# Attention and two feed-forward layers on one core: weight conversions moved between steps, key slots laid out anew

## The chip, the cores and the metric

The kernel runs on one core of a Trainium2 chip. The metric is the device time of one execution in microseconds (us). Before the change the median of three runs is 629.02 us (628.22 to 630.41).

## What is computed

Attention with a window and sinks, then two feed-forward layers, each over the 1536 tokens that the one before gives (2 batches of 768):

```python
scores = scale * np.matmul(q, k.transpose(0, 1, 3, 2))
keep = (pos[None, :] < n_sink) | ((rel >= 0) & (rel < window))
scores = np.where(keep, scores, -1e9); a = softmax(scores)
x = np.matmul(a, v)                       # 8 heads of 64, written as [1536, 512]
x = softplus(x @ w_in) @ w_out            # 512 -> 2048 -> 512
y = ((h := x @ w2_in) * np.clip(h + 3, 0, 6) / 6) @ w2_out
```

With the inputs, n_sink is 4 and window is 128. The weights arrive as 64-bit floats.

## The kernel before

**Attention.** The tokens are cut into 12 groups g of 128 (i = g % 6 within a batch), and the 8 heads into two quads. Step n of the loop at L603 handles group n // 2, quad n % 2, for n from 0 to 23; steps 24 to 26 finish what is in flight. Work is a pipeline: step n issues the scores of n on TensorE (PE), the transposes of the probabilities of n-1, on odd steps the transposes of a finished group's output (`turn_x`), and the products with the values of n-2 (`apply`). VectorE (DVE) adds the mask and takes the minimum (`exps`, L500), ScalarE (ACT) exponentiates, and DVE and ACT copy transposed probabilities out of PSUM (`copies`). A group's output is divided by its sums (`normalise`, DVE, L557), turned (PE) and stored as a high part (ACT, L568) and a low part (DVE, L572), since the feed-forward products take each factor as a sum of two parts.

**Keys.** `keys` holds for each block i one slot of 144 columns: 64 keys, 16 columns for the sinks, 64 keys. A query row needs the last 64 keys of the block before, its own block and the sinks, and for half of the rows the first 64 keys of the block before. `spread_sinks` (GpSimd, POOL) copies the sinks to all slots once per batch. Blocks with i == 0 need no block before; their scores are taken in halves of 64 keys (L480).

**Weights.** A "half" (`Weights.half`, L87) converts one 512 KB piece of a weight matrix from 64-bit to two 32-bit parts: three DVE instructions (L97, L100, L103), one on ACT (L107), one on POOL (L108). `fetch` keeps up to four pieces loading ahead. `HALVES` says behind which steps a half is put: steps 3, 5 to 23, eleven in all. The names are w_c_io, c the column block of 128, io 0 for w_in and 1 for w_out.

**Feed-forward.** Steps 24 to 26 already hold the first-layer products of column blocks c = 0, 1 and 2 for tokens 0 to 511 (`products`, 12 matmuls of 512 columns each). `activate` (softplus, L155) runs over ACT, POOL and DVE; its DVE instruction L175 sets the PSUM buffer of the product free, of which there are three. `stage_b` (L188) multiplies with w_out, again 12 matmuls. From `ffn.run` on, `filler` puts the rest of the halves behind the activations of c = 4 to 14.

**What sets the order.** The whole part up to `ffn.run(0, FIXED)` stands under `in_order`: each engine executes its instructions in the order in which the program writes them. So a DVE instruction that waits holds all DVE work behind it. Loads go out on SyncE's queue (SP) in program order, each one waiting until the load eight places ahead has landed.

Of the kernel before, what the change touches and what calls it, by code (L numbers as in the profile page):

```python
# [8 lines left out]
F32 = mybir.dt.float32  # L9
# [5 lines left out]
ALU = mybir.AluOpType  # L15
# [3 lines left out]
P = 128  # L19
NEG = 1.0e9  # L20
MAXSINK = 16
HQ = P // 2
SLOTW = P + MAXSINK
YW = HQ + MAXSINK
PW = P + YW
TB = 2
HALVES = (3, 5, 7, 9, 11, 13, 15, 17, 19, 21, 23)
WARM = 22
FIXED = 4

# [338 lines left out]
def banded_attention(ctx, tc, qT_d, kT_d, v, ident, NSv, Wv, xT, psa, isq, w, ffn, flags):  # L369


    nc = tc.nc
    B, H, D, S = qT_d.shape
# [3 lines left out]
    NQ = 2 * NG  # L377
# [10 lines left out]
    def fetch(g):  # L388
        b, i = divmod(g, NB)
        s = st.setdefault(g, {})  # L390
        s["q"] = thr.tile([P, NP, P], F32, tag="q", name=f"q_{g}")
        for ps in (slice(0, NP),) if g else (slice(0, NP // 2), slice(NP // 2, NP)):
            for t, src, eng in ((0, qT_d, nc.sync), (1, kT_d, nc.sync if g else nc.scalar)):
                src = src[b].rearrange("(p t) d s -> (t d) p s", t=2)[:, ps, i * P : (i + 1) * P]
                if t == 0:
                    eng.dma_start(s["q"][:, ps], src)
                else:
                    for r in range(2):
                        c0 = r * (HQ + MAXSINK)
                        eng.dma_start(keys[:, ps, i, c0 : c0 + HQ], src[:, :, r * HQ : (r + 1) * HQ])  # L400

    def fetch_v(g):
        b, i = divmod(g, NB)
        s = st.setdefault(g, {})
        s["vx"] = thr.tile([P, H, D], F32, tag="vx", name=f"vx_{g}")
        lo = i * P - (HQ if i else 0)
        nc.sync.dma_start(s["vx"], v[b, lo : lo + P])
        if i:
            s["vy"] = thr.tile([YW, 2, H, D], F32, tag="vy", name=f"vy_{g}")
            lo = (i - 1) * P  # L410
            nc.sync.dma_start(s["vy"][0:HQ, 0], v[b, lo : lo + HQ])
            nc.sync.dma_start(s["vy"][HQ:YW, 0], v[b, 0:MAXSINK])
            lo = i * P + HQ
            nc.sync.dma_start(s["vy"][0:MAXSINK, 1], v[b, 0:MAXSINK])
            nc.sync.dma_start(s["vy"][MAXSINK:YW, 1], v[b, lo : lo + HQ])

    def spread_sinks():

        nc.gpsimd.tensor_copy(
            keys[:, :, :, HQ : HQ + MAXSINK],  # L420
            keys[:, :, 0:1, 0:MAXSINK].to_broadcast([P, NP, NB, MAXSINK]),
        )

# [12 lines left out]
    def masks(i):  # L436

        if i == 0:
            nc.vector.tensor_scalar(out=mt[:, 0:P], in0=rmc, scalar1=0.0, scalar2=hid, op0=ALU.is_lt, op1=ALU.mult)
            nc.vector.tensor_scalar(out=m_zero, in0=rmc, scalar1=Wv, scalar2=hid, op0=ALU.is_ge, op1=ALU.mult)  # L440
            nc.vector.tensor_tensor(out=m_zero, in0=m_zero, in1=mt[:, 0:P], op=ALU.min)
            nc.vector.tensor_scalar(out=mS, in0=col, scalar1=NSv, scalar2=None, op0=ALU.is_ge)
            nc.vector.tensor_tensor(out=m_zero, in0=m_zero, in1=mS, op=ALU.mult)
        elif i == 1:
            nc.vector.tensor_scalar(out=mt, in0=rel, scalar1=0.0, scalar2=hid, op0=ALU.is_lt, op1=ALU.mult)
            nc.vector.tensor_scalar(out=m_gen, in0=rel, scalar1=Wv, scalar2=hid, op0=ALU.is_ge, op1=ALU.mult)
            nc.vector.tensor_tensor(out=m_gen, in0=m_gen, in1=mt, op=ALU.min)
            for r, c0 in ((r0, P + HQ), (r1, P)):
                nc.vector.tensor_scalar(
                    out=m_gen[r, c0 : c0 + MAXSINK], in0=mS[r, 0:MAXSINK], scalar1=hid, scalar2=None, op0=ALU.mult  # L450
                )
            nc.vector.tensor_copy(m_one, m_gen)
            nc.vector.tensor_tensor(
                out=m_one[r0, P : P + HQ], in0=m_gen[r0, P : P + HQ], in1=mS[r0, 0:HQ], op=ALU.mult
            )
            nc.vector.memset(m_one[r0, P + HQ : PW], hid)

    def scores(n):
        g, quad = divmod(n, 2)
        i = g % NB  # L460
        s = st[g]
        if quad == 0:
            s["sum"] = two.tile([P, H], F32, tag="sum", name=f"sum_{g}")
            s["mx"] = two.tile([P, H], F32, tag="mx", name=f"mx_{g}")
        s["P", quad] = two.tile([P, 4, PW], F32, tag="P", name=f"P_{n}")
        s["s", quad] = [psa.tile([P, 2, 256], F32, tag="s", name=f"s_{n}_{t}") for t in range(2)]
        for pp in range(2):
            p = quad * 2 + pp
            if i == 0:
                parts = [None]  # L470
            else:
# [104 lines left out]
    def keep_busy(n):  # L576
# [17 lines left out]
    nc.vector.tensor_scalar(out=rel[:, 0:P], in0=rmc, scalar1=float(HQ), scalar2=None, op0=ALU.add)
    nc.vector.tensor_scalar(
        out=rel[r0, P : P + HQ], in0=rmc[r0, 0:HQ], scalar1=float(P), scalar2=None, op0=ALU.add
    )
    nc.vector.memset(rel[r0, P + HQ : PW], 0.0)
    nc.vector.memset(rel[r1, P : P + MAXSINK], 0.0)
    nc.vector.tensor_scalar(  # L600
        out=rel[r1, P + MAXSINK : PW], in0=rmc[r1, 0:HQ], scalar1=float(-HQ), scalar2=None, op0=ALU.add
    )
    for n in range(NQ + 3):  # L603
        g, quad = divmod(n, 2)
        new, old, older = n < NQ, 0 <= n - 1 < NQ, 0 <= n - 2 < NQ
        late = n >= NQ
        ready = n // 2 - 2 if n % 2 == 0 and n >= 4 else None
        turned = (n - 5) // 2 if n % 2 and n >= 5 else None
        if new:
            scores(n)  # L610
        else:
            ffn.products("w1", 0, n - NQ)
        if n == 0:
            keep_busy(6)
        if old:
            transposes(n - 1)
        if turned is not None:
            turn_x(turned)
        if older:
            apply(n - 2)  # L620
        if late and ready is not None:
            normalise(ready)
        if new:
            for hh in range(4):
                exps(n, hh)
        if old:
            copies(n - 1, nc.vector)
            copies(n - 1, nc.scalar)
        if ready is not None and not late:
            normalise(ready)  # L630
        if turned is not None:
            store_hi(turned)
        if ready is not None and ready >= 1:
            store_lo(ready - 1)
        if n % 2 == 0 and n >= 2 and n // 2 - 1 < NG:
            inverse(n // 2 - 1)
        if quad == 1 and new:
            if g % NB == 0:
# [133 lines left out]
```

## Time and profile before

| | |
|---|---|
| median of 3 runs | 629.02 us |
| the profiled execution | 628.13 us, span 626.3 us |
| PE matmul busy | 611.6 us, 98% of the span, 3804 instructions |
| DVE / ACT / POOL busy | 322.6 / 329.1 / 206.2 us |
| mean granted TensorE clock | 0.992 |
| L145 and L202, the feed-forward products | 1152 matmuls each, 283.7 and 281.9 us |
| DMA | 50.16 MB; 46603 packets, 15249 of them under 512 B |

Busy is the time an engine spends in instructions, as a sum. The span is the profiled execution from its first to its last instruction, and the time has about 1.8 us around it. PE is almost always busy, so time can be won only where PE waits, where its clock is lower, or where it does work that can be left out.

### The profile page before, as it was taken

What the parts mean: (1) busy time and instruction counts of PE and PEld (TensorE: products, weight loads), DVE (VectorE), ACT (ScalarE), POOL (GpSimd) and SP (SyncE); (2) the same over time, 40 slices, a digit from 0 to 9 for tenths busy, and PEclk for the clock granted to TensorE, in tenths of its full rate; (3) what the DMA queues carried; (4) which work ended last, traced back from release to release, by engine and by line L of the source; (5) the groups of instructions that cost most, each with busy time, mean ns of one, the idle gap of its engine ahead of it and who ended that gap; (6) DMA issues with size and microseconds to landing.
All of it is one profiled execution on the core that took longest, in us unless ns stands there. A gap on an engine that the chain in (4) does not pass through costs nothing.

```text
span 626.3 us, 10133 instructions
## 1 busy us (share of the span) xinstructions
PE 611.6 (98%) x3804; PEld 503.3 (80%) x3804; DVE 322.6 (51%) x693; ACT 329.1 (53%) x715; POOL 206.2 (33%) x170
## 2 busy tenths in 40 slices
PE   9799999899999999999999999999999999999996
PEld 5688887688888888888888888888888888888884
DVE  5699976998424222256999984222322222322221
ACT  4698986787668566566878743222222222322221
POOL 1111215898644444446899941000000000000000
PEclk9899999899999999999999999999999999999998
DMA  7999979100000000025665520000100000100001
GB/s 191 277 282 248 261 250 324 69 1 1 1 1 1 0 1 0 2 75 176 213 197 181 168 67 2 1 1 1 67 1 1 1 0 1 67 1 1 1 1 72
DMA packets 46603, 50.16 MB, mean 80 GB/s; under 512 B 15249, under 2 KB 37777, under 8 KB 46545
## 3 DMA queue, kind: packets, MB, share of 16 engines
q1 hardware_dynamic: 45312, 49.16, 25.5%
q8 instruction: 32, 0.52, 0.3%
q10 hardware_dynamic: 1232, 0.26, 0.2%
q14 instruction: 27, 0.21, 0.1%
HBM read 46.27 MB, written 3.15 MB: 79 GB/s over the span
## 4 chain that ended last, share of the span: by engine, by line
PE 87%; DMA 4%; ACT 3%; DVE 2%; SPq 2%; issue 1%; ACTq 0%; DVEq 0%
PE h_w L145 41%; PE y_w L202 40%; PE pt L518 2%; PE o L542 2%; ACT P L504 2%; DMA raw_w<-in_moe_w_out_dram 1%; DMA vx<-in_v_dram 1%; PE s L487 1%; DMA q<-in_q_dram 1%; DMA raw_w<-in_moe_w_in_dram 1%; DVE xs L500 1%; PE xtr L565 1%; DMA vy<-in_v_dram 0%; ACT w_w L107 0%; PE s L480 0%
## 5 line engine op out<-in xcount | busy, mean ns | idle before, releaser
L145 PE MATMUL h_w<-xT,w_w 128*128 128x512 f32 x1152 | 283.7, 391 | 2.8 <-DVE e_w L175 2.8
L145 PEld LDWEIGHTS h_w<-xT,w_w 128*128 128x128 f32 x1152 | 216.9, 189 | 49.2 <-DVE e_w L175 3.9
L202 PE MATMUL y_w<-g_w,w_w 128*128 128x512 f32 x576 | 143.0, 389 | 0.0
L202 PE MATMUL y_w<-w_w,g_w 128*128 128x512 f32 x576 | 138.9, 389 | 0.0
L202 PEld LDWEIGHTS y_w<-w_w,g_w 128*128 128x128 f32 x576 | 107.9, 188 | 23.2 <-ACT g_w L182 0.4
L202 PEld LDWEIGHTS y_w<-g_w,w_w 128*128 128x128 f32 x576 | 108.0, 188 | 22.8 <-DVE xT L572 0.5
L108 POOL TENSOR_TENSOR w_w<-t_w,w_w 128x512 fp32r<-128x512 f32 x64 | 82.8, 1296 | 88.1 <-ACT w_w L107 82.9
L181 DVE SCALAR_TENSOR_TENSOR h_w<-e_w,h_w 128x512 f32<-128x512 f32 x48 | 33.4, 695 | 89.0 <-ACT e_w L179 89.0
L179 ACT ACTIVATE e_w<-h_w 128x512 f32<-128x512 f32 x48 | 28.7, 599 | 96.0 <-PE h_w L145 94.6
L182 ACT ACTIVATE g_w<-h_w 128x512 fp32r<-128x512 f32 x48 | 28.7, 598 | 91.2 <-PE y_w L202 91.0
L183 DVE SCALAR_TENSOR_TENSOR g_w<-h_w,g_w 128x512 fp32r<-128x512 f32 x48 | 33.2, 691 | 83.7 <-ACT g_w L182 83.7
L171 POOL TENSOR_TENSOR u_w<-u_w,e_w 128x512 f32<-128x512 f32 x48 | 62.1, 1293 | 43.1 <-ACT u_w L170 41.0
L177 POOL TENSOR_TENSOR g_w<-e_w,g_w 128x512 fp32r<-128x512 f32 x48 | 62.1, 1295 | 38.8 <-ACT g_w L176 38.1
L174 DVE SCALAR_TENSOR_TENSOR h_w<-h_w,r_w 128x512 f32<-128x512 f32 x48 | 33.4, 696 | 55.9 <-ACT r_w L172 55.7
L504 ACT ACTIVATE P<-xs,mx 128x208 f32<-128x208 f32 (+1 forms) x96 | 42.6, 447 | 12.5 <-DVE mx L500 12.3
L175 DVE TENSOR_TENSOR e_w<-h_w,u_w 128x512 f32<-128x512 f32 x48 | 33.0, 687 | 31.1 <-POOL u_w L171 30.9
L167 ACT ACTIVATE e_w<-h_w 128x512 f32<-128x512 f32 x48 | 28.4, 592 | 37.1 <-PE h_w L145 31.8
L107 ACT ACTIVATE w_w<-t_w 128x512 fp32r<-128x512 f32 x64 | 39.9, 623 | 13.9 <-DVE t_w L103 13.7
L176 ACT ACTIVATE g_w<-e_w 128x512 fp32r<-128x512 f32 x48 | 30.0, 624 | 26.6 <-DVE e_w L175 16.7
L97 DVE TENSOR_SCALAR m_w<-raw_w 128x512 int32<-128x512 int32 x53 | 36.7, 692 | 8.0 <-DMA raw_w<-in_moe_w_in_dram 3.8
L103 DVE SCALAR_TENSOR_TENSOR t_w<-raw_w,m_w 128x512 int32<-128x512 int32 x53 | 36.2, 683 | 2.9
L100 DVE SCALAR_TENSOR_TENSOR m_w<-raw_w,m_w 128x512 int32<-128x512 int32 x53 | 36.6, 691 | 1.0
(74 smaller groups left out, 452.0 us busy)
## 6 DMA issues: line engine op xcount, KB each, us to landing
raw_w<-in_moe_w_in_dram SPq DMA_DIRECT2D x32, 512.0 KB, 4.4
raw_w<-in_moe_w_out_dram SPq DMA_DIRECT2D x32, 512.0 KB, 4.6
vx<-in_v_dram SPq DMA_DIRECT2D x12, 256.0 KB, 5.2
out_dram<-o SPq DMA_DIRECT2D x12, 256.0 KB, 2.1
q<-in_q_dram SPq DMA_DIRECT2D x11, 256.0 KB, 4.8
keys<-in_k_dram SPq DMA_DIRECT2D x22, 128.0 KB, 4.4
vy<-in_v_dram SPq DMA_DIRECT2D x20, 128.0 KB, 4.6
vy<-in_v_dram SPq DMA_DIRECT2D x20, 32.0 KB, 4.7
```

The lines of the kernel that those rows point to most:

```text
L97: nc.vector.tensor_scalar(out=m, in0=hi, scalar1=3, scalar2=0x3FFFFFF8, op0=ALU.logical_shift_left, op1=ALU.bitwise_and)
L100: nc.vector.scalar_tensor_tensor(out=m, in0=hi, scalar=-0x40000000, in1=m, op0=ALU.bitwise_and, op1=ALU.bitwise_or)
L103: nc.vector.scalar_tensor_tensor(out=t, in0=lo, scalar=29, in1=m, op0=ALU.logical_shift_right, op1=ALU.bitwise_or)
L107: nc.scalar.activation(wt[:, 0, :], t.bitcast(F32), AF.Copy)
L108: nc.gpsimd.tensor_tensor(out=wt[:, 1, :], in0=t.bitcast(F32), in1=wt[:, 0, :].bitcast(F32), op=ALU.subtract)
L145: nc.tensor.matmul(h, wt[:, ws, kk * P : (kk + 1) * P], xT[:, xs, kk, t0 : t0 + 512], start=(n == 0), stop=(n == 11),)
L171: nc.gpsimd.tensor_tensor(out=u, in0=u, in1=e, op=ALU.subtract)
L174: nc.vector.scalar_tensor_tensor(out=h, in0=h, scalar=0.0, in1=r, op0=ALU.max, op1=ALU.add)
L177: nc.gpsimd.tensor_tensor(out=glo, in0=e, in1=ghi.bitcast(F32), op=ALU.subtract)
L181: nc.vector.scalar_tensor_tensor(out=h, in0=e, scalar=6.0, in1=h, op0=ALU.min, op1=ALU.mult)
L202: ins = nc.tensor.matmul(y, lhsT, rhs, start=(c == 0 and n == 0), stop=(c == 15 and n == 2))
L504: nc.scalar.activation(s["P", quad][:, hh, 0:w_], xs, AF.Exp, scale=-1.0, bias=s["mx"][:, h : h + 1], accum_out=s["sum"][:, h : h + 1],)
```

## The change

The key slots become 128 keys and then 16 columns for sinks, so the keys of a block are one load and one matmul operand; masks, `rel` and the value rows are put in the matching order (`vx` and `vy` then come in six loads of a group where there were five). The first half moves from step 3 to step 5, step 24 gets one half and steps 25 and 26 two each; in those last steps the halves stand ahead of `exps` and, at step 26, ahead of `normalise`. The second softplus (c = 1) moves from `ffn.run` into step 25.

```diff
+XW = P + MAXSINK
-HALVES = (3, 5, 7, 9, 11, 13, 15, 17, 19, 21, 23)
+HALVES = (5, 7, 9, 11, 13, 15, 17, 19, 21, 23, 24, 25, 25, 26, 26)
...
-                    for r in range(2):
-                        c0 = r * (HQ + MAXSINK)
-                        eng.dma_start(keys[:, ps, i, c0 : c0 + HQ], src[:, :, r * HQ : (r + 1) * HQ])
+                eng.dma_start(keys[:, ps, i, 0:P] if t else s["q"][:, ps], src)
...
+        nc.sync.dma_start(s["vx"][0:HQ], v[b, t0 - HQ : t0])
+        nc.sync.dma_start(s["vx"][HQ:YW], v[b, 0:MAXSINK])
+        nc.sync.dma_start(s["vx"][YW:P], v[b, t0 : t0 + P - YW])
+        nc.sync.dma_start(s["vy"][0:MAXSINK, 0], v[b, t0 + P - YW : t0 + HQ])
+        nc.sync.dma_start(s["vy"][MAXSINK:YW, 0], v[b, t0 - P : t0 - HQ])
+        nc.sync.dma_start(s["vy"][:, 1], v[b, t0 + P - YW : t0 + P])
...
-            for r, c0 in ((r0, P + HQ), (r1, P)):
-                nc.vector.tensor_scalar(
-                    out=m_gen[r, c0 : c0 + MAXSINK], in0=mS[r, 0:MAXSINK], scalar1=hid, scalar2=None, op0=ALU.mult
-                )
+            nc.vector.tensor_scalar(
+                out=m_gen[:, HQ:YW], in0=mS[:, 0:MAXSINK], scalar1=hid, scalar2=None, op0=ALU.mult
+            )
...
-                parts = [(r0, HQ + MAXSINK, P, 0), (r1, HQ + MAXSINK, PW, 0), (r0, 0, YW, P)]
+                parts = [(r0, HQ, XW, 0), (r1, HQ, PW, 0), (r0, 0, HQ, XW)]
...
-                        for j in range(2):
-                            c0 = j * (HQ + MAXSINK)
-                            nc.tensor.matmul(
-                                ps[:, pp, j * HQ : (j + 1) * HQ], s["q"][rows, p, :],
-                                keys[rows, p, 0, c0 : c0 + HQ], start=True, stop=True,
-                            )
+                        nc.tensor.matmul(
+                            ps[:, pp, 0:P], s["q"][rows, p, :], keys[rows, p, 0, 0:P], start=True, stop=True
+                        )
...
+        if n == NQ:
+            normalise(ready)
+        if late:
+            for _ in range(HALVES.count(n)):
+                w.half()
+        if n > NQ and ready is not None:
             normalise(ready)
...
-        if n == NQ:
-            ffn.activate("w1", "softplus", 0, 0, lambda: None)
-        if n in HALVES:
+        if late and n < NQ + 2:
+            ffn.activate("w1", "softplus", 0, n - NQ, lambda: None)
+        if n in HALVES and new:
             w.half()
```

DVE's order around the first half before (xs and mx: the masked scores of a step; PT: transposed probabilities; raw_w and t_w: a piece of weights as loaded and converted; m_one and m_gen: masks):

```order
L525 COPY PT_0_365<-pt_0_335 128x256
L97 TENSOR_SCALAR t_w_0_0_381<-raw_w_0_0_257 128x512
L100 SCALAR_TENSOR_TENSOR t_w_0_0_381<-raw_w_0_0_257,t_w_0_0_381 128x512
L103 SCALAR_TENSOR_TENSOR t_w_0_0_381<-raw_w_0_0_257,t_w_0_0_381 128x512
L500 ISA xs_0_434,mx_391<-s_0_393,m_gen 128x208
```

The half of w_0_0 stood between the copy of step 3 and the scores of step 4. Now, at the same place and up to the half behind step 5:

```order
L516 COPY PT_0_353<-pt_0_323 128x256
L491 ISA xs_0_413,mx_370<-s_0_372,m_gen 128x208
...
L516 COPY PT_0_425<-pt_0_386 128x256
L548 TENSOR_TENSOR x_430<-o_275,rs_299 128x512
...
L516 COPY PT_0_493<-pt_0_450 128x256
L98 TENSOR_SCALAR t_w_0_0_510<-raw_w_0_0_245 128x512
L101 SCALAR_TENSOR_TENSOR t_w_0_0_510<-raw_w_0_0_245,t_w_0_0_510 128x512
```

The whole of steps 4 and 5 now stands ahead of it. DVE's order in steps 24 to 26 before (h, e: softplus of the product named; x: a group's divided output; xtr: it turned):

```order
L175 TENSOR_TENSOR e_w_0_0_1883<-h_w_0_0_1831,u_w_0_0_1885 128x512
L557 TENSOR_TENSOR x_1944<-o_1854,rs_1879 128x512
L572 TENSOR_TENSOR xT<-xtr_1909,xT 128x4x128
L572 TENSOR_TENSOR xT<-xtr_1947,xT 128x4x128
L97 TENSOR_SCALAR m_w_6_0_2075<-raw_w_6_0_1402 128x512
```

And now, from the same softplus to the last group's output (of each half the first and the last of three instructions):

```order
L176 TENSOR_TENSOR e_w_0_0_1863<-h_w_0_0_1802,u_w_0_0_1865 128x512
L98 TENSOR_SCALAR t_w_6_0_1910<-raw_w_6_0_1520 128x512
...
L98 TENSOR_SCALAR t_w_5_1_1919<-raw_w_5_1_1660 128x512
...
L175 SCALAR_TENSOR_TENSOR h_w_0_1_1876<-h_w_0_1_1876,r_w_0_1_1929 128x512
L176 TENSOR_TENSOR e_w_0_1_1928<-h_w_0_1_1876,u_w_0_1_1930 128x512
L98 TENSOR_SCALAR t_w_7_0_1954<-raw_w_7_0_1800 128x512
...
L98 TENSOR_SCALAR t_w_6_1_1961<-raw_w_6_1_1851 128x512
...
L548 TENSOR_TENSOR x_1968<-o_1825,rs_1859 128x512
L563 TENSOR_TENSOR xT<-xtr_1889,xT 128x4x128
```

Four halves and the softplus of c = 1 moved ahead of the last x. On PE, the order at this place, which the change leaves as it was:

```order
L146 MATMUL h_w_0_2_1941<-xT,w_w_2_0_961 128x512 x12
L556 MATMUL xtr_1971<-ident,x_1968 128x128 x4
L203 MATMUL y_w_0_0_2012<-g_w_0_0_1862,w_w_0_1_810 128x512 x3
L203 MATMUL y_w_0_1_2016<-g_w_0_0_1862,w_w_0_1_810 128x512 x3
L203 MATMUL y_w_0_2_2020<-g_w_0_0_1862,w_w_0_1_810 128x512 x3
```

The turning of that x stands between the products of c = 2 and the first output products y.

## Rows read from the trace of the kernel before

**Rows 1.** The page, the chain that ended last: shares of the span by engine.
```profile
PE 87%; DMA 4%; ACT 3%; DVE 2%; SPq 2%; issue 1%; ACTq 0%; DVEq 0%
```
**Rows 2.** Busy time by stretch, granted clock, DMA share, for two stretches of attention.
```profile
core 0: us, PE busy (x) PEld busy (x) DVE busy (x) ACT busy (x) POOL busy (x), PEclk, DMA share, GB/s
20.00:40.00 20.00, 16.36 (x303) 14.04 (x300) 16.91 (x66) 15.57 (x55) 3.84 (x3) 0.91 0.98 285
...
60.00:80.00 20.00, 19.07 (x392) 16.78 (x392) 19.39 (x80) 19.15 (x70) 3.84 (x3) 1.00 0.96 261
```
**Rows 3.** Timeline of DVE, first half: start, us, instruction, [idle before, releaser].
```profile
21.36 0.43 DVE L97 TENSOR_SCALAR t_w<-raw_w 128x512 int32<-128x512 int32 x1 [3.81 <-DMA raw_w<-in_moe_w_in_dram]
```
**Rows 4.** Timeline of PE: scores of steps 4, 5 (second part), 6 and 8.
```profile
17.30 0.93 PE L487 MATMUL s<-keys,q 64*64 64x128 f32 x24
...
24.27 0.93 PE L487 MATMUL s<-keys,q 64*64 64x128 f32 x22 [3.57 <-DVE mx L500]
...
29.28 0.94 PE L487 MATMUL s<-keys,q 64*64 64x128 f32 x24
...
35.66 0.93 PE L487 MATMUL s<-keys,q 64*64 64x128 f32 x24
```
**Rows 5.** Busy time by stretch, behind PE's two waits (columns as in rows 2).
```profile
26.00:28.00 2.00, 2.00 (x11) 1.57 (x12) 1.97 (x9) 2.00 (x8) 0.00 (x0) 0.50 1.10 304
121.00:124.00 3.00, 3.00 (x8) 2.30 (x7) 2.86 (x5) 2.12 (x5) 3.00 (x4) 0.50 0.01 3
```
**Rows 6.** Timelines at the start: PE's first scores, DVE's first exps, a mask.
```profile
7.76 1.16 PE L480 MATMUL s<-keys,q 64*128 64x64 f32 x16
...
8.90 0.29 DVE L500 CUSTOM_DVE_ANT_0 xs<-s,m_zero 128x128 f32<-128x128 f32 x1 [1.35 <-PE s L480]
...
10.70 0.35 DVE L449 TENSOR_SCALAR m_gen<-mS 64x16 f32<-64x16 f32 x2
```
**Rows 7.** Timeline of SP: key loads of groups 1 and 4 issued.
```profile
4.66 1.54 SPq L400 DMA_DIRECT2D keys<-in_k_dram  x2
...
26.44 2.76 SPq L400 DMA_DIRECT2D keys<-in_k_dram  x2
```
**Rows 8.** The page, DMA issues: count, KB each, us to landing.
```profile
keys<-in_k_dram SPq DMA_DIRECT2D x22, 128.0 KB, 4.4
```
**Rows 9.** Timeline of DVE, steps 23 to 26.
```profile
86.44 0.42 DVE L97 TENSOR_SCALAR t_w<-raw_w 128x512 int32<-128x512 int32 x1
...
88.23 0.68 DVE L557 TENSOR_TENSOR x<-o,rs 128x512 f32<-128x512 f32 x1
90.90 0.43 DVE L525 COPY PT<-pt 128x256 f32<-128x256 f32 x1 [2.00 <-PE pt L518]
...
96.10 0.69 DVE L175 TENSOR_TENSOR e_w<-h_w,u_w 128x512 f32<-128x512 f32 x1
96.86 0.69 DVE L557 TENSOR_TENSOR x<-o,rs 128x512 f32<-128x512 f32 x1
```
**Rows 10.** Timelines of ACT and POOL: the softplus of c = 1.
```profile
100.24 0.60 ACT L568 ACTIVATE xT<-xtr 128x512 fp32r<-128x512 f32 x1 [2.30 <-PE xtr L565]
100.74 0.59 ACT L167 ACTIVATE e_w<-h_w 128x512 f32<-128x512 f32 x1
...
103.23 0.62 ACT L172 ACTIVATE r_w<-e_w 128x512 f32<-128x512 f32 x1
...
103.40 1.29 POOL L171 TENSOR_TENSOR u_w<-u_w,e_w 128x512 f32<-128x512 f32 x1 [4.57 <-ACT u_w L170]
```
**Rows 11.** Timeline of PE, step 26 and the first column blocks behind it.
```profile
96.74 3.02 PE L145 MATMUL h_w<-xT,w_w 128*128 128x512 f32 x12
99.61 0.60 PE L565 MATMUL xtr<-ident,x 128*128 128x128 f32 x4
...
120.11 4.63 PE L145 MATMUL h_w<-xT,w_w 128*128 128x512 f32 x12 [2.45 <-DVE e_w L175]
```
**Rows 12.** The chain that ended last, in order of time: twelve matmuls at the full clock.
```profile
132.23 2.72 PE h_w L145 x12
```

More of the change, by code (lines that the diff above doesn't have):

```diff
@@ L394, in fetch @@
                 src = src[b].rearrange("(p t) d s -> (t d) p s", t=2)[:, ps, i * P : (i + 1) * P]
-                if t == 0:
-                    eng.dma_start(s["q"][:, ps], src)
-                else:
-                    for r in range(2):
-                        c0 = r * (HQ + MAXSINK)
-                        eng.dma_start(keys[:, ps, i, c0 : c0 + HQ], src[:, :, r * HQ : (r + 1) * HQ])
+                eng.dma_start(keys[:, ps, i, 0:P] if t else s["q"][:, ps], src)
     def fetch_v(g):
@@ L405, in fetch_v @@
         s["vx"] = thr.tile([P, H, D], F32, tag="vx", name=f"vx_{g}")
[L406 to L415, printed above, removed]
+        if i == 0:
+            nc.sync.dma_start(s["vx"], v[b, 0:P])
+            return
+        t0 = i * P
+        s["vy"] = thr.tile([YW, 2, H, D], F32, tag="vy", name=f"vy_{g}")
+        nc.sync.dma_start(s["vx"][0:HQ], v[b, t0 - HQ : t0])
[4 more added lines that the diff above has]
+        nc.sync.dma_start(s["vy"][:, 1], v[b, t0 + P - YW : t0 + P])
     def spread_sinks():
         nc.gpsimd.tensor_copy(
-            keys[:, :, :, HQ : HQ + MAXSINK],
+            keys[:, :, :, P:SLOTW],
             keys[:, :, 0:1, 0:MAXSINK].to_broadcast([P, NP, NB, MAXSINK]),
@@ L447, in masks @@
             nc.vector.tensor_tensor(out=m_gen, in0=m_gen, in1=mt, op=ALU.min)
-            for r, c0 in ((r0, P + HQ), (r1, P)):
-                nc.vector.tensor_scalar(
-                    out=m_gen[r, c0 : c0 + MAXSINK], in0=mS[r, 0:MAXSINK], scalar1=hid, scalar2=None, op0=ALU.mult
-                )
+            nc.vector.tensor_scalar(
+                out=m_gen[:, HQ:YW], in0=mS[:, 0:MAXSINK], scalar1=hid, scalar2=None, op0=ALU.mult
+            )
             nc.vector.tensor_copy(m_one, m_gen)
-            nc.vector.tensor_tensor(
-                out=m_one[r0, P : P + HQ], in0=m_gen[r0, P : P + HQ], in1=mS[r0, 0:HQ], op=ALU.mult
-            )
-            nc.vector.memset(m_one[r0, P + HQ : PW], hid)
+            nc.vector.tensor_tensor(out=m_one[r0, XW:PW], in0=m_gen[r0, XW:PW], in1=mS[r0, 0:HQ], op=ALU.mult)
+            nc.vector.memset(m_one[r0, HQ:YW], hid)
     def scores(n):
@@ L477, in scores @@
                     if i == 0:
-                        for j in range(2):
-                            c0 = j * (HQ + MAXSINK)
-                            nc.tensor.matmul(
-                                ps[:, pp, j * HQ : (j + 1) * HQ], s["q"][rows, p, :],
-                                keys[rows, p, 0, c0 : c0 + HQ], start=True, stop=True,
-                            )
+                        nc.tensor.matmul(
+                            ps[:, pp, 0:P], s["q"][rows, p, :], keys[rows, p, 0, 0:P], start=True, stop=True
+                        )
                     else:
@@ L592, in banded_attention @@
     fetch(2)
[L594 to L602, printed above, removed]
+    nc.vector.tensor_scalar(out=rel[:, 0:HQ], in0=rmc[:, 0:HQ], scalar1=float(HQ), scalar2=None, op0=ALU.add)
+    nc.vector.memset(rel[:, HQ:YW], 0.0)
+    nc.vector.tensor_copy(rel[:, YW:XW], rmc[:, 0:HQ])
+    for r, by in ((r0, float(P)), (r1, float(-HQ))):
+        nc.vector.tensor_scalar(out=rel[r, XW:PW], in0=rmc[r, 0:HQ], scalar1=by, scalar2=None, op0=ALU.add)
     for n in range(NQ + 3):
@@ L620, in banded_attention @@
             apply(n - 2)
-        if late and ready is not None:
+        if n == NQ:
[4 more added lines that the diff above has]
+        if n > NQ and ready is not None:
             normalise(ready)
```

## The prediction

> **What bounds the kernel.** I read the chain of waits first: 87% of it is TensorE (PE) [rows 1], so only PE's waits, its half-clock stretches and its own work count. Next the busy time by stretch. From 20 to 40 us PE is busy 16.36 of 20 us at a mean granted clock of 0.91, while the DMA engines are busy 0.98 of the time; from 60 to 80 us DVE (19.39) and ACT (19.15) are as full as PE (19.07) [rows 2]. So early attention loses time, and later attention has three engines in balance. Then the timelines of the two places that the change touches.
>
> First place: DVE stands 3.81 us before the first conversion, until its raw weights land [rows 3]. DVE is in order, so the masks of step 4 wait behind it; PE can't go on with the scores of step 5 and idles 3.57 us [rows 4]. Behind that wait the clock is at 0.50, the lower of its two levels, 1.2 GHz [rows 5]. Second place: column block 6 (L145) waits 2.45 us for DVE's softplus, because 21 conversions still have to go between the softpluses, and its twelve matmuls then take 4.63 us at the low clock [rows 11], where twelve take 2.72 [rows 12].
>
> **The start of attention.** Without the conversion, step 4's masks can follow its scores at once. Steps 4 and 5 are then like any pair; from step 6 to step 8 a pair takes 35.66 - 29.28 = 6.38 us [rows 4]. So step 6 starts near 17.30 + 6.38 = 23.7, plus 0.1 for the conversion that stays in step 5, against 29.28: 5.5 us won, the low clock's share included. Bounds: 3.57 (the idle time alone) and 5.6. The weights aren't late again: they landed at 21.36 at the latest [rows 3], and step 5 reaches its conversion near 22.9, half a pair and its own masks later.
>
> **Keys in one operand.** The scores of blocks with i = 0 go from 16 matmul passes to 8 in four steps (0, 1, 12, 13). Sixteen take 1.16 us [rows 6]; halving all of it would save 0.58 a step, and if passes of 128 columns take twice as long, nothing. At step 0 DVE waits for these scores [rows 6]; in step 0's masks one small instruction of two falls away, 0.17 us. I take 0.6 us there (0.2 to 0.8). At steps 12 and 13 PE gets ahead, but DVE and ACT are nearly full behind it [rows 2]: 0.3 us (0 to 1.1). The other scores keep 416 columns per head pair (144 + 208 + 64 for 128 + 208 + 80): nothing. Masks and `rel` are otherwise the same sizes: nothing. Loads: one key load fewer and one value load more per group, the same bytes; rows of keys are 512 B rather than 256. The loads run ahead of their use, so I cost them at nothing; if that cover fails, see the first rival. The 512 KB load of w_8_0, which SP issued early, now comes late: fewer bytes in the full stretch. **Attention wins 5.5 + 0.6 + 0.3 = 6.4 us** (3.8 to 7.5).
>
> **Its end.** I follow it on the clock of the trace before. A conversion takes DVE 88.23 - 86.44 = 1.79 us [rows 9]. The one added at step 24 fits: DVE idles 2.00 us ahead of the copy at 90.90 [rows 9]. ACT's part of it has the same gap. The four of steps 25 and 26 stand, with the second softplus between the pairs, ahead of the last group's x:
>
> - The first softplus ends on DVE at 96.10 + 0.69 = 96.8, where x followed at once [rows 9].
> - Two conversions: 3.58, to 100.4. ACT converts the second piece, stores an x (0.50 from one start to the next [rows 10]), about 101.4.
> - ACT's softplus: its last step began 2.49 us behind its first, POOL's part another 0.17 behind that and takes 1.29 [rows 10]: 105.4.
> - DVE's second instruction (0.69, the next starts 0.6 later): 106.0. Two conversions: 109.6. x, 0.69 [rows 9]: 110.3.
>
> PE ends the products of block 2 at 99.6 and then needs that x; before it had it [rows 11]. In order, it cannot take the output products that stand behind. **It waits 99.6 to 110.3: 10.7 us, a new wait.** Bounds: 10 and 11.5, from rounding and from ACT's and POOL's conversions meeting. Nothing covers it.
>
> What comes back: 15 conversions are done, not 11, so 17 go between the softpluses where 21 did. DVE needs 17/11 x 2.1 + 1.3 = 4.6 us per column block, PE 24 matmuls = 5.4 us; before it was 21/11, or 5.3, next to nothing to spare. The wait at block 6 and what hangs on it go. To compare, I take the start of block 6 as if PE ran on at full clock. Before: 120.11 + (4.63 - 2.72) = 122.0 [rows 11, 12]. Now: 110.3 + 0.53 for the turning, then six runs of twelve matmuls (three outputs, three products), 6 x 2.72 = 16.3 [rows 12]: 127.2, plus the low clock behind the new wait. Each of the two waits was followed by a stretch at 0.50 [rows 5]; the measured cost of one is 1.9 us, and I take 1.8. Bounds: nothing, and 3.8 for two. So 129.0 - 122.0: **the end loses 7.0 us** (4.5 to 9.8).
>
> The Trainium skill's page "TensorE: Matmul & The Clock Gate" (section "HAM oscillation — how this bites in real kernels") speaks against the change: idle gaps in the matmul stream make the work behind them start cold, so such gaps should be closed, not opened; in its example about 1.67 us are throttled behind each gap, half of it lost. The trace agrees on the mechanism (clock 0.50 behind both waits), but one stretch cost 1.9 us here, not 0.8; by the page's figure, as an estimate, the sum below would come out 1.0 us lower.
>
> **Sum.** -6.4 + 7.0 = +0.6 us on the profiled execution's 628.13 us: 628.7. That execution was 0.9 below the median of the runs shown, so against the median: **629.6 us**. What a measurement of this kernel can tell from no change is about 0.3%, 1.9 us: 627.1 to 630.9. Two large terms cancel; the forecast is no change, and its own range 627.6 to 631.0.
>
> **Rivals.**
> 1. *Slower: the loads become the bound.* Attention starts 6 us earlier from step 6 on, but the DMA engines are already 0.98 busy there [rows 2]. SP's key load for group 4 (used at step 8) was issued at 26.44 to 29.2 [rows 7] and takes 4.4 us to land [rows 8], so 32.5 to 33.2, where step 8 came at 35.66 [rows 4] and now comes near 29.6. For the change: 512 KB less ahead of it, at 285 GB/s [rows 2] 1.8 us, and the key load of group 1 is issued up to 2 us earlier, since it no longer waits at 4.66 [rows 7]. That leaves it at about 29, a tie. It decides if it lands after 29.6. Price: 1.5 us late plus a low clock of 1.8: 632.9 us. Chance 0.15.
> 2. *Slower: the end costs more.* Two stretches of low clock behind the long wait, or conversions that overlap on DVE, ACT and POOL and take longer: +2 us, 631.6 us. For it: the wait is three times longer than those before. Against: a single stretch followed both of these. Chance 0.13.
> 3. *Faster: the wait costs less and the keys more is won.* Low clock near the lower bound (0.5 lost), attention at its upper bound of 7.5: 110.3 + 0.53 + 16.3 + 0.5 - 122.0 - 7.5 = -1.9, 627.1 us; also if PE's steady steps shrink with the scores. Against: DVE and ACT are full there. Chance 0.20.
> 4. *The change doesn't do what it says:* the first conversion still waits at step 5. It would need the load to come 1.5 us later than before, while less stands ahead of it. Within the first rival's chance.
>
> **How the numbers follow.** No change has 0.52, the first two rivals 0.28 together, the third 0.20. Leaving out the outermost tenth on each side, the range is 627.0 to 632.8: down to the third rival, up to nearly the first.
>
> **What would show it.** Right: no wait of DVE for raw weights before 30 us; step 6's scores near 23; the first feed-forward product near 81 rather than 87.34; then PE idle near 10.7 us ahead of the last turning, released by DVE's x, followed by a clock of 0.50; no wait of a product for L175/L176 afterwards. Wrong: a PE idle time below 8 us at the end, which means that x doesn't stand behind all four conversions in time; a start of the first product later than 83, which means that loads or another engine hold the loop; or further waits of column blocks 5 to 8.

## The result: 637.09 us, slower by 1.2%, outside the range

The changed kernel took 637.09 us in the median of four runs (635.61 to 637.72), the kernel before 628.96 beside it: ratio 1.0123, interval 1.0097 to 1.0149. The forecast was 629.6 (627.0 to 632.8). The profiled executions differ by 635.61 - 628.13 = 7.5 us. The views of the changed kernel follow in the order of the rows of before.

The page, shares of the chain that ended last by engine, and busy time by stretch (columns as in [rows 2]):

```profile
PE 87%; DVE 6%; DMA 3%; SPq 1%; ACT 1%; issue 1%; POOL 0%; DVEq 0%
```

```profile
20.00:40.00 20.00, 18.35 (x374) 16.49 (x370) 17.14 (x70) 17.62 (x62) 2.55 (x2) 1.00 0.82 245
60.00:80.00 20.00, 19.43 (x410) 17.43 (x406) 19.47 (x80) 19.38 (x70) 4.54 (x4) 1.00 0.95 256
...
110.00:112.00 2.00, 0.36 (x2) 0.37 (x3) 2.00 (x3) 0.63 (x1) 0.71 (x2) 0.50 0.00 0
112.00:116.00 4.00, 4.00 (x16) 3.34 (x15) 2.62 (x5) 3.12 (x6) 0.99 (x1) 0.68 0.75 239
```

DVE rose from 2% of the chain to 6%. From 20 to 40 us PE is busy 18.35 instead of 16.36 us and the clock stays at 1.00, but not all of the 20 us is won. Behind the long wait the clock is at 0.50, as behind both waits of before [rows 5].

DVE's first conversion, and PE at the places of [rows 4] and [rows 11]:

```profile
22.82 0.42 DVE L98 TENSOR_SCALAR t_w<-raw_w 128x512 int32<-128x512 int32 x1
```

```profile
23.60 0.94 PE L478 MATMUL s<-keys,q 64*64 64x144 f32 x24
...
31.77 1.05 PE L478 MATMUL s<-keys,q 64*64 64x144 f32 x24 [1.65 <-DMA keys<-in_k_dram]
...
45.85 0.81 PE L472 MATMUL s<-keys,q 64*128 64x128 f32 x8 [0.99 <-DMA keys<-in_k_dram]
...
83.89 3.06 PE L146 MATMUL h_w<-xT,w_w 128*128 128x512 f32 x12
...
93.33 3.01 PE L146 MATMUL h_w<-xT,w_w 128*128 128x512 f32 x12
111.64 1.11 PE L556 MATMUL xtr<-ident,x 128*128 128x128 f32 x4 [15.29 <-DVE x L548]
112.40 3.97 PE L203 MATMUL y_w<-g_w,w_w 128*128 128x512 f32 x12
```

The conversion doesn't wait any more, and step 6 starts at 23.60 instead of 29.28. But PE waits for keys at steps 8 and 12, so the first feed-forward product starts only 3.45 us earlier (87.34 before). Then it stands 15.29 us ahead of the last turning. From there to the end nothing waits.

Loads on SP, to be read against [rows 7]:

```profile
18.44 0.43 SPq L80 DMA_DIRECT2D raw_w<-in_moe_w_in_dram  x1
...
26.46 0.39 SPq L396 DMA_DIRECT2D q<-in_q_dram  x1
28.29 0.39 SPq L396 DMA_DIRECT2D keys<-in_k_dram  x1
```

The keys of group 4 go out at 28.29, eight loads behind the weight piece of 18.44, whose landing they wait for; step 8 needed them at 30.12.

DVE and POOL, first at the conversion of step 24 and then between the first softplus and the last x:

```profile
85.99 1.66 DVE L101 SCALAR_TENSOR_TENSOR t_w<-raw_w,t_w 128x512 int32<-128x512 int32 x1
...
93.66 0.69 DVE L176 TENSOR_TENSOR e_w<-h_w,u_w 128x512 f32<-128x512 f32 x1
94.27 0.42 DVE L98 TENSOR_SCALAR t_w<-raw_w 128x512 int32<-128x512 int32 x1
94.72 0.69 DVE L101 SCALAR_TENSOR_TENSOR t_w<-raw_w,t_w 128x512 int32<-128x512 int32 x1
95.45 1.66 DVE L104 SCALAR_TENSOR_TENSOR t_w<-raw_w,t_w 128x512 int32<-128x512 int32 x1
97.03 0.41 DVE L98 TENSOR_SCALAR t_w<-raw_w 128x512 int32<-128x512 int32 x1
...
98.20 1.63 DVE L104 SCALAR_TENSOR_TENSOR t_w<-raw_w,t_w 128x512 int32<-128x512 int32 x1
...
104.83 0.69 DVE L176 TENSOR_TENSOR e_w<-h_w,u_w 128x512 f32<-128x512 f32 x1
...
106.61 1.63 DVE L104 SCALAR_TENSOR_TENSOR t_w<-raw_w,t_w 128x512 int32<-128x512 int32 x1
108.17 0.41 DVE L98 TENSOR_SCALAR t_w<-raw_w 128x512 int32<-128x512 int32 x1
...
109.34 1.63 DVE L104 SCALAR_TENSOR_TENSOR t_w<-raw_w,t_w 128x512 int32<-128x512 int32 x1
110.90 0.68 DVE L548 TENSOR_TENSOR x<-o,rs 128x512 f32<-128x512 f32 x1
```

```profile
85.80 1.30 POOL L109 TENSOR_TENSOR w_w<-t_w,w_w 128x512 fp32r<-128x512 f32 x1 [5.22 <-ACT w_w L108]
...
95.09 1.46 POOL L178 TENSOR_TENSOR g_w<-e_w,g_w 128x512 fp32r<-128x512 f32 x1 [1.47 <-ACT g_w L177]
97.85 1.44 POOL L109 TENSOR_TENSOR w_w<-t_w,w_w 128x512 fp32r<-128x512 f32 x1 [1.29 <-ACT w_w L108]
...
106.26 1.44 POOL L178 TENSOR_TENSOR g_w<-e_w,g_w 128x512 fp32r<-128x512 f32 x1 [1.47 <-ACT g_w L177]
108.99 1.44 POOL L109 TENSOR_TENSOR w_w<-t_w,w_w 128x512 fp32r<-128x512 f32 x1 [1.29 <-ACT w_w L108]
```

The third instruction of each of the four conversions ahead of x takes 1.63 to 1.66 us, and so does the second of the one of step 24, where the same form takes 0.69 elsewhere. Each begins while an instruction of POOL runs and ends some 0.55 us behind POOL's end. The groups of instructions of DVE show it as a mean: the form with the intermediate in t_w, in attention, and with it in m_w, in the feed-forward part (count | busy, mean ns).

```profile
L104 DVE SCALAR_TENSOR_TENSOR t_w<-raw_w,m_w 128x512 int32<-128x512 int32 x49 | 33.5, 684 | 3.1
L104 DVE SCALAR_TENSOR_TENSOR t_w<-raw_w,t_w 128x512 int32<-128x512 int32 x15 | 14.2, 945 | 0.5
```

In the kernel before, where no conversion of attention ran beside an instruction of POOL, the second form had 692 ns:

```profile
L103 DVE SCALAR_TENSOR_TENSOR t_w<-raw_w,t_w 128x512 int32<-128x512 int32 x11 | 7.6, 692 | 0.4
```

### The profile page after: what moved, and what is told of

It is laid out like the page before. It is cut to its first block, busy times and chain, and to the rows that moved or that the text cites. A ratio compares the mean times of both kernels' runs of the same rounds, so it can differ in the third digit from the quotient of the medians.

```text
span 633.8 us, 10061 instructions
## 1 busy us (share of the span) xinstructions
PE 607.7 (96%) x3772; PEld 501.3 (79%) x3772; DVE 327.6 (52%) x692; ACT 330.9 (52%) x715; POOL 206.9 (33%) x170
## 4 chain that ended last, share of the span: by engine, by line
PE 87%; DVE 6%; DMA 3%; SPq 1%; ACT 1%; issue 1%; POOL 0%; DVEq 0%
PE y_w L203 41%; PE h_w L146 40%; DMA vx<-in_v_dram 2%; DMA raw_w<-in_moe_w_out_dram 1%; DVE t_w L104 1%; PE pt L509 1%; PE spare L570 1%; DVE xs L491 1%; DVE t_w L101 1%; PE s L478 1%; PE o L533 1%; DVE x L548 1%; DVE t_w L98 0%; POOL u_w L172 0%; SPq L396 0%
## 5 line engine op out<-in xcount | busy, mean ns | idle before, releaser
L98 DVE TENSOR_SCALAR m_w<-raw_w 128x512 int32<-128x512 int32 x49 | 33.9, 692 | 7.7 <-DMA raw_w<-in_moe_w_in_dram 3.8
L104 DVE SCALAR_TENSOR_TENSOR t_w<-raw_w,m_w 128x512 int32<-128x512 int32 x49 | 33.5, 684 | 3.1
L101 DVE SCALAR_TENSOR_TENSOR m_w<-raw_w,m_w 128x512 int32<-128x512 int32 x49 | 33.8, 691 | 0.9
```

Of the source, the lines that this page charges most:

```text
L98: nc.vector.tensor_scalar(out=m, in0=hi, scalar1=3, scalar2=0x3FFFFFF8, op0=ALU.logical_shift_left, op1=ALU.bitwise_and)
L101: nc.vector.scalar_tensor_tensor(out=m, in0=hi, scalar=-0x40000000, in1=m, op0=ALU.bitwise_and, op1=ALU.bitwise_or)
L104: nc.vector.scalar_tensor_tensor(out=t, in0=lo, scalar=29, in1=m, op0=ALU.logical_shift_right, op1=ALU.bitwise_or)
```

## The experiments

Times are medians, ratios are to the kernel before run beside them; the waits are PE's, of the profiled execution. "Turning" is the wait ahead of the last one, "blocks 5, 6" the waits of products for a softplus. A profile shows one execution, and a median can lie off it: the changed kernel's profiled execution (635.61) was the fastest of its four.

| run | us | ratio (interval) | keys | first product | turning | blocks 5, 6 |
|---|---|---|---|---|---|---|
| before | 628.96 | 1 | 0 | 87.34 | 0 | 0.35, 2.45 |
| the change | 637.09 | 1.0123 (1.0097 to 1.0149) | 1.65, 0.99 | 83.89 | 15.29 | 0 |
| first_half_at_5 | 625.93 | 0.9949 (0.9932 to 0.9965) | 2.49 | 87.98 | 0.45 | 0.34, 2.46 |
| keys_alone | 628.29 | 0.9998 (0.9985 to 1.0010) | 0 | 88.15 | 0 | 2.48 at 6 |
| x_not_behind | 626.31 | 0.9967 (0.9956 to 0.9978) | 3.58 | 86.10 | 0 | 0.37, 2.47 |
| mid_psum | 634.25 | 1.0090 (1.0069 to 1.0110) | 2.46 | 84.78 | 12.36 | 0 |
| softplus_back | 631.34 | 1.0050 (1.0034 to 1.0067) | 0.56 | 82.48 | 9.62 | 0 |
| two_ahead | 636.81 | 1.0121 (1.0097 to 1.0145) | 0 | 85.91 | 14.32 | 0 |
| two_ahead_again | 635.59 | 1.0103 (1.0061 to 1.0146) | 0 | 81.87 | 15.28 | 0 |
| half_after_x | 623.49 | 0.9929 (0.9909 to 0.9950) | 1.53 | 83.51 | 0 | 0.36, 2.47 |
| half_after_x_two_ahead | 623.93 | 0.9934 (0.9918 to 0.9951) | 0 | 82.95 | 0 | 0.35, 2.43 |
| old_keys_twelve | 624.84 | 0.9925 (0.9899 to 0.9951) | 0.7 | 83.49 | 0.45 | 0 |
| fixed_5 | 624.10 | 0.9922 (0.9896 to 0.9949) | 2.71 | 84.08 | 0 | 0.17 at 7 |
| three_ahead | 624.33 | 0.9922 (0.9904 to 0.9940) | 1.52, 0.86, 0.60 | 83.55 | 0 | 0.34, 2.45 |

### The start alone, and the keys alone

```diff
 first_half_at_5, to the kernel before:
-HALVES = (3, 5, 7, 9, 11, 13, 15, 17, 19, 21, 23)
+HALVES = (5, 7, 9, 11, 13, 15, 17, 19, 21, 23, 24)
 keys_alone: the change without its edits to HALVES and to the steps from 24 on
```

> The kernel before with the first conversion behind step 5, and one behind the softplus of step 24 in its place; keys and all else as before. Theory (the start gains about 5.5 us, and then the key load of group 4 comes late because it is issued only when the weight loads ahead of it have landed, whatever the layout): step 6 starts near 24 us instead of 29.28, step 8 waits 1 to 3 us for keys, the first feed-forward product starts at 83 to 85 us instead of 87.34; the wait of the product of column block 6 stays; 624 to 626 us. Rival (the new key layout made the keys late): no wait for keys at step 8, first product near 82 us, about 623 us.

> The kernel before with the new key slots, masks and value loads alone. Theory: the scores of blocks with i = 0 are shorter, which gives 0 to 1 us; the first conversion waits for its weights as before (3.8 us) and the time is 628 to 629 us. Rival (six value loads per group in place of five, some of 32 KB, hold up the weights and keys behind them): the first weights land over 1 us later than before's 21.36, and the time is 630 us or more.

In first_half_at_5, with the old keys, PE waited at step 8 too (timeline of PE):

```profile
33.84 1.78 PE L487 MATMUL s<-keys,q 64*64 64x128 f32 x24 [2.49 <-DMA keys<-in_k_dram]
```

So the late keys don't come from the new layout: that rival falls. Its scores behind the wait ran at the low clock (1.78 us, 0.93 in [rows 4]), and this execution was its slowest, 629.0, where the other four took 624.93 to 626.11; its first product came at 87.98, not at 83 to 85 as expected. In keys_alone the first conversion waited 3.88 us, until 22.04 (21.36 in [rows 3]), and the time is the same (ratio 0.9985 to 1.0010): the layout neither wins nor loses anything that can be measured.

### What stands ahead of the last x

```diff
 x_not_behind, to the change:
-HALVES = (5, ..., 23, 24, 25, 25, 26, 26)
+HALVES = (5, ..., 23, 24)
-        if late and n < NQ + 2:
+        if n == NQ:
 softplus_back, to the change: the second of these edits alone
 mid_psum, to the change, for the conversions of steps 24 to 26:
+            w.mid = pso.tile([P, 512], I32, tag="o", name="mid")
...
-        m = self.psum.tile(...) if self.psum else t
+        m = self.psum.tile(...) if self.psum else (self.mid or t)
```

> The changed kernel without the four conversions of steps 25 and 26 and with the second softplus back behind the last turning, so that nothing but the first softplus stands ahead of the last x on VectorE. Theory (the 15.3 us that TensorE waits are those conversions and that softplus): the wait ahead of the last turning falls below 1 us; the start stays as in the changed kernel (first product near 83.9 us); the wait of a product for the softplus at column blocks 5 to 7 returns with 2 to 4 us and a stretch of low clock behind it; 624 to 627 us. Rival (the loss lies elsewhere, in loads or in the clock): 631 us or more.

> The changed kernel with the second softplus back behind the last turning; the four conversions of steps 25 and 26 stay ahead of the last x. Theory (the wait is the sum of what stands ahead of x on VectorE, conversions and softplus): four conversions, each held up once by GpSimd, 4 x 2.73 = 10.9 us behind the first softplus, so TensorE waits 9 to 10.5 us ahead of the last turning instead of 15.3; one to two of that may come back as a wait of the second output product for its softplus; 631 to 633.5 us. Rival (the softplus, with its way over three engines, is most of the wait): the wait falls to 4 to 7 us, below 629 us.

> The changed kernel, in whose conversions of steps 24 to 26 the intermediate word m lies in a PSUM buffer, as it does in the feed-forward part, and not in the SBUF tile t. Theory (a VectorE instruction with both inputs in SBUF waits for the GpSimd instruction beside it; five of 1.63 to 1.66 us instead of 0.69 in the changed kernel): no instruction of these conversions takes over 0.8 us; the first of a conversion takes 0.69 instead of 0.42; the wait of TensorE ahead of the last turning falls from 15.3 to 12 to 13.5 us, the time by 2 to 3 us, to about 634.5. Rival (those instructions are long for another reason, such as the copy on ScalarE that reads the tile): the wait stays at 15 us or more, 637 us.

Without anything ahead of x the wait is gone and the time falls by 637.09 - 626.31 = 10.8 us; the waits of blocks 5 and 6 come back. The start was to stay that of the change and didn't: PE waited 3.58 us for keys, and the first product came at 86.10.

With the four conversions but without the softplus the wait is 9.62 us, 5.67 less, and the time falls by 5.75. That the two agree is in part luck. Between the profiled executions the time falls by 635.61 - 631.04 = 4.57, though the first product also came 1.41 us earlier; so 2.5 us were lost again behind the turning, 0.8 of them in the first output product (twelve matmuls took 4.78 us at the low clock instead of 3.97). Where the rest went was not traced.

In mid_psum, timelines of DVE, POOL and PE:

```profile
96.11 0.69 DVE L105 SCALAR_TENSOR_TENSOR t_w<-raw_w,mid 128x512 int32<-128x512 int32 x1
...
98.29 0.69 DVE L105 SCALAR_TENSOR_TENSOR t_w<-raw_w,mid 128x512 int32<-128x512 int32 x1
```

```profile
95.49 1.30 POOL L179 TENSOR_TENSOR g_w<-e_w,g_w 128x512 fp32r<-128x512 f32 x1 [1.47 <-ACT g_w L178]
97.54 1.27 POOL L110 TENSOR_TENSOR w_w<-t_w,w_w 128x512 fp32r<-128x512 f32 x1 [0.75 <-ACT w_w L109]
```

```profile
109.55 1.12 PE L557 MATMUL xtr<-ident,x 128*128 128x128 f32 x4 [12.36 <-DVE x L549]
```

Same instructions, same POOL work beside them, one input now in PSUM: 0.69 us each, though the first of a conversion takes 0.69 instead of 0.42. The wait falls by 2.9 us and the time by 2.8 (by 1.4 between the profiled executions: in that of mid_psum the keys came 0.8 us later, and the first output product took 4.69 us instead of 3.97). So the long instructions were DVE waiting for POOL because both inputs lay in SBUF; the rival (ScalarE's copy) falls. The Trainium skill's page "SBUF — State Buffer" (section "Who interferes with whom") says as much: a VectorE instruction with two SBUF inputs contends with a GpSimd instruction that reads SBUF, and the pair of ports that the two share is locked by one of them. The trace agrees: 0.69 became 1.63 to 1.66, and POOL's took 1.44 to 1.46 where it began beside such an instruction of DVE, against 1.30.

### The keys of group 4

```diff
 two_ahead, to the change (two_ahead_again is the same kernel):
-        w = Weights(nc, ..., 4)
+        w = Weights(nc, ..., 2)
+        if n in (13, 17):
+            w.ahead += 1
```

> The changed kernel with two weight pieces loading ahead instead of four until step 13, three until step 17, then four. Theory (the keys of groups 4 and 6 are late because their loads are issued and carried behind weight pieces that nobody needs yet): TensorE waits less than 0.3 us for keys at steps 8 and 12 (1.65 and 0.99 in the changed kernel), the first feed-forward product starts near 81.3 us instead of 83.9, and the time falls by 2 to 3 us, to about 634.5; the wait ahead of the last turning stays at 15 to 15.5 us. Rival (the queues are full with keys and values alone): the waits for keys stay, 637 us; or conversions now wait for their weights at steps 7 to 23.

> two_ahead once more. There the wait for keys was gone, but in the profiled execution TensorE stood 2.36 us at step 23 with nothing in the trace that it waited for, and the time was no better. Theory (the loads that now come later hold up something at step 23, always in the same place): the same stand of 2 to 2.5 us at step 22 or 23, 636 to 637 us. Rival (chance, a single execution): no such stand, first feed-forward product near 82 us, 634 to 635 us.

With two pieces ahead PE never waits for keys, in three kernels (half_after_x_two_ahead too): the cause is shown. How long the wait is varies between executions: five traces with the same loads up to group 4's keys (the change, mid_psum, softplus_back, half_after_x, fixed_5) have 0.56 to 2.71 us. The time didn't follow in two_ahead: 636.81. In its profiled execution PE stood in the middle of step 23 (timeline of PE, and busy time by stretch):

```profile
79.45 0.44 PE L509 MATMUL pt<-ident,P 128*128 128x128 f32 x2
82.24 1.44 PE L509 MATMUL pt<-ident,P 128*128 128x128 f32 x6 [2.36 <-issue]
```

```profile
80.00:82.00 2.00, 0.00 (x0) 0.00 (x0) 1.01 (x8) 1.84 (x8) 0.00 (x0) 0.97 0.98 322
82.00:84.00 2.00, 1.76 (x9) 1.67 (x9) 1.10 (x3) 0.68 (x3) 0.00 (x0) 0.50 0.79 217
```

"issue" means that it waited for nothing that the profile shows; the DMA engines were 0.98 busy, and the one 16 KB load of instructions of these microseconds began only at 79.62, 2.62 us before PE went on. In two_ahead_again this load began at 76.80 (the one before it at 68.3, here at 68.1), and there is no such stand. Two shorter stands on "issue" also ended that long behind the beginning of such a load: in first_half_at_5 (0.45 us) 2.36 us behind, in old_keys_twelve (0.16 us) 2.59. So PE probably waited for its own instructions; no run tests it. In two_ahead_again the first product starts at 81.87, and that execution took 633.63, 2.0 less than the change's; the other of its two runs took 637.55. So the stand isn't always there, as its rival said, though the median missed the rival's 634 to 635. What delays the other executions was not traced.

### Versions that beat both

```diff
 half_after_x, to x_not_behind: one more conversion, behind the last x
-HALVES = (5, ..., 23, 24)
+HALVES = (5, ..., 23, 24, 26)
...
-        if n == NQ:
-            normalise(ready)
         if late:
+            if ready is not None:
+                normalise(ready)
             for _ in range(HALVES.count(n)):
                 w.half()
-        if n > NQ and ready is not None:
-            normalise(ready)
 half_after_x_two_ahead: with the edits of two_ahead; three_ahead: with 3, and 4 from step 17 on
 fixed_5: half_after_x with FIXED = 5
 old_keys_twelve: first_half_at_5 with 26 added to HALVES
```

> The kernel without the conversions and the softplus ahead of x (x_not_behind), with one conversion more behind the last x in step 26, where VectorE is idle. Theory (the wait of column block 6 for the softplus is VectorE's backlog of conversions, and one conversion of about 2.2 us less takes away most of it): the waits of block 5 and 6, 0.37 and 2.47 us, fall together below 1 us, and with the low clock behind them 2.5 to 4 us go: 622.5 to 624 us. Rival (the wait is set by the order of the conversions between the softpluses, not by their number): it stays above 2 us, 626 us.

> The kernel before (old key slots) with first_half_at_5's steps and one conversion more, behind the last x in step 26; with twelve conversions in attention the load of w_8_0 is no longer issued at step 1, and between any two softpluses of column blocks 1 to 5 there stand two conversions (before: three between those of blocks 2 and 3). Theory (half_after_x won by the load that no longer stands ahead of group 4's keys, and the wait of column block 6 comes from the three conversions between two softpluses): the wait for keys at step 8 falls from 2.5 to 1.7 us or less, the wait of block 6 below 0.7 us, 620.5 to 623 us. Rival (the new key layout carried the gain): 625 us or more.

> half_after_x with FIXED at 5, so that the conversions are put behind the activations from column block 5 on; three conversions now stand first between the softpluses of blocks 3 and 4 rather than 2 and 3. Theory (those three make the wait of block 6): no wait at block 6 over 0.7 us, one of 0 to 1.5 us at block 7, and 621 to 622.5 us. Rival (the backlog of conversions as a whole makes the wait): 2 us or more of wait at block 6 or 7, 623.5 us.

> half_after_x with the loads of two_ahead. Theory: both gains add up: no wait for keys at step 8 (3.6 us of wait in x_not_behind), no wait of block 6 over 1 us: 618 to 621 us. Rival (fewer weights ahead makes the later conversions, or the feed-forward ones, wait for their loads): 623 us or more.

> half_after_x with three weight pieces loading ahead until step 17, then four. Theory (each piece of 512 KB ahead of group 4's keys delays them by 1.8 us): no wait for keys at step 8 (1.5 us in half_after_x), and 621.5 to 622.5 us, unless another load comes late. Rival (as with two pieces ahead, what the keys win is lost again between steps 8 and 23): 623 to 624.5 us.

half_after_x came out in its range, but not by its theory: the wait of block 6 stayed. Product 6 in x_not_behind, then in half_after_x (timelines of PE):

```profile
118.91 4.26 PE L146 MATMUL h_w<-xT,w_w 128*128 128x512 f32 x12 [2.47 <-DVE e_w L176]
```

```profile
117.75 3.01 PE L146 MATMUL h_w<-xT,w_w 128*128 128x512 f32 x12 [2.47 <-DVE e_w L176]
```

What it won lies elsewhere, ahead of block 6 and in the clock: with twelve conversions in attention the load of w_8_0 is no longer pulled forward to step 1, ahead of group 4's keys (SP's weight loads at 18 us, x_not_behind, then half_after_x).

```profile
18.34 1.17 SPq L80 DMA_DIRECT2D raw_w<-in_moe_w_in_dram  x2
```

```profile
18.88 0.43 SPq L80 DMA_DIRECT2D raw_w<-in_moe_w_in_dram  x1
```

The wait for keys fell from 3.58 to 1.53, and the wait of block 6 was not followed by the low clock (3.01 us for twelve, not 4.26). old_keys_twelve agrees: the same twelve with the old keys, wait for keys 0.7 instead of 2.49, and with the old layout the same ratio, so that rival falls, though its time lay above the forecast 620.5 to 623. How much of the gain is the keys' isn't settled: the load of w_8_0 explains the direction, but with the same loads fixed_5 waited 2.71. The other part is the clock: the eight executions of x_not_behind had a mean granted clock of 0.989 to 0.994, the four of half_after_x 0.997 to 1.000. And the conversion behind the last x isn't free: in half_after_x the first output product waited 0.96 + 0.25 us for the low part of x.

The wait of block 6 is one for the softplus of block 3. Three conversions in a row, between the softpluses of blocks 2 and 3, are a part of it. That softplus in half_after_x, fixed_5 and old_keys_twelve (timelines of DVE):

```profile
117.01 0.68 DVE L176 TENSOR_TENSOR e_w<-h_w,u_w 128x512 f32<-128x512 f32 x1
```

```profile
115.45 0.68 DVE L176 TENSOR_TENSOR e_w<-h_w,u_w 128x512 f32<-128x512 f32 x1
```

```profile
117.02 0.68 DVE L175 TENSOR_TENSOR e_w<-h_w,u_w 128x512 f32<-128x512 f32 x1
```

In fixed_5, where the three come one block later, it ends 32.1 us behind the first product instead of 34.2, PE comes to block 6 1.0 us later, and the wait is gone. In old_keys_twelve, with two conversions between each, it ends no earlier (34.2): there the wait is gone because PE came later to block 6, after an output product had waited 2.73 us for the low part of x behind the added conversion. Neither gained by it, and both missed their times: in fixed_5 the second output product waited 0.48 + 0.86 us for its softplus, beside 2.71 for keys. half_after_x_two_ahead and three_ahead missed their times: fewer pieces ahead moved the late loads (three waits of 1.52, 0.86 and 0.60 in three_ahead) rather than removing them. In half_after_x_two_ahead the late load is a weight piece, as its rival said: a conversion waits 1.18 us for it, until 37.66, and PE stands 0.83 us behind that; its first product comes only 0.56 us earlier than in half_after_x. All five lie at 0.992 to 0.993 of the kernel before and can't be told apart.

## Why the prediction was wrong, step by step

- **The start: right.** 5.5 us up to step 6, and 0.6 for shorter scores; measured 29.28 - 23.60 = 5.7 together. How much of it is the shorter scores' isn't shown: keys_alone, where they stand alone, took as long as the kernel before. From step 12 to the first product it took 83.89 - 45.85 = 38.04 us instead of 38.79 (48.55 to 87.34): 0.75 won where 0.3 was forecast, behind a wait for keys that gave DVE and ACT time.
- **"The loads run ahead of their use, so I cost them at nothing": wrong.** The text named this as the first rival, with a chance of 0.15, put the landing of group 4's keys at 29, and called it a tie. The load was issued at 28.29 and PE waited 1.65 us; group 6's keys cost another 0.99. The start won 3.45 us, not 6.4. The prediction's own sign of loads that hold the loop came, a first product later than 83 (83.89). The row for it was there: a load that is issued only when the one eight places ahead has landed doesn't come earlier because its user does.
- **The wait ahead of the last turning: right in kind, too small.** 10.7 us forecast, 15.29 measured. The step that failed is "Two conversions: 3.58": with POOL beside it one takes 97.03 - 94.27 = 2.76, or 110.90 - 108.17 = 2.73, and all four were hit: 4 x (2.74 - 1.79) = 3.8 us. The first softplus came another 1.0 late (94.35, where 96.8 - 3.45 = 93.35 was forecast), behind the conversion of step 24, which was to fit and which POOL held up too; in mid_psum, where it isn't held up, the first softplus is still half of that late. Together 4.8, near the 4.6 missing. In the kernel before no conversion of attention ran beside POOL, so its row gave the price without a collision, and the bound of 11.5 "from conversions meeting" had no row behind it. The second rival named conversions that overlap and take longer, at +2 us and with a chance of 0.13: the right mechanism at less than half its price. POOL's 1.29 us [rows 10] would have been the bound: each of four conversions later by up to that.
- **The low clock behind it: right.** 0.5 for the turning (1.11 instead of 0.60) and 1.1 for the first output (3.97 instead of 2.88): 1.6 where 1.8 was taken.
- **No product waits afterwards: right, but not for the reason given** (17 conversions instead of 21). The changed kernel has three conversions between the softpluses of blocks 2 and 3 too, and these end 8.3 us apart (before 8.2). But DVE did the second softplus (104.83) while PE stood, and the softplus of block 3 ended at 126.6, where PE came to block 6 only at 129.8. In a version with 20 conversions left, half_after_x, the wait of block 6 was the same 2.47 us as with 21. So what decides, by these traces, is how far DVE is ahead of PE there; the number of conversions by itself was not tested.
- **The sum.** Reckoned as the prediction did, six runs of twelve behind the last turning end at 127.09 + 2.72 = 129.8, on the clock of before 129.8 + 3.45 = 133.3 against 122.0: the end lost 11.3 us, not 7.0. And 11.3 - 3.45 = 7.8, against 7.5 measured between the executions. x_not_behind agrees: its profiled execution took 635.61 - 627.06 = 8.55 us less than the change's, though its first product came 2.21 us later, which makes 10.8 for what stands ahead of x.
- **The range** reached up to a late key load alone. The key loads and the conversions that meet were both on the slow side, and both came, so 632.8 was too low by 4.3.

What stays open: the other three executions of the changed kernel took 636.69 to 637.72 at a mean granted clock below the profiled one's (0.982 to 0.985 against 0.989); where they lost it was not traced. The profiled execution of mid_psum, at 0.984, shows places where it can be lost: behind its wait for keys the scores took 1.78 us instead of 1.05, and its first output product 4.69 instead of 3.97.

## What to carry to other kernels

Before work of VectorE is moved next to work of GpSimd, look where its inputs lie: an instruction with two inputs in SBUF took 1.63 to 1.66 us there instead of 0.69, and with one of them in PSUM 0.69 again. A wait that is taken out of the start uncovers the next queue: ask of every load behind it when it is issued, not when it is used. Filling an idle time of an in-order engine is free only if nothing that another engine needs stands behind the filling: one conversion behind the last x is part of a version at 0.993 of the time before and made an output product wait 1.2 us, four ahead of it cost PE a wait of 9.6 us.

## What the runs showed of the hardware that was not expected

- Even a small instruction is caught by POOL, and one that reads a single tensor from SBUF: this one, 0.16 us by itself, took 1.21 beside POOL's 1.29, in the changed kernel (timeline of DVE), in x_not_behind and in mid_psum alike.

```profile
89.22 1.21 DVE L542 TENSOR_SCALAR rs<-sum 128x8 f32<-128x8 f32 x1
```

- The same wait of PE, 2.4 to 2.5 us ahead of product 6, was followed by twelve matmuls at the low clock in four profiled executions (4.26 to 4.63 us) and at the full clock in three (3.01 to 3.06). Of four waits for keys of 2.46 to 3.58 us three were followed by a stretch at the low clock, and one (2.71, in fixed_5) was not.
- PE stood 2.36 us with no wait that the profile names in one execution of two_ahead and not in the other; in the one with the stand a 16 KB load of instructions began 2.8 us later than in the other (79.62 against 76.80), while the DMA engines were 0.98 busy. That the two belong together is likely and not shown.
